# Attention rows of two steps turned together, and the first pair's second-layer weights asked for ahead of the half tile's

## The chip, the core and the metric

The kernel runs on one NeuronCore of a Trainium2 chip (trn2). The metric is the time of one execution in device microseconds. The core has five engines with queues of their own: PE (matrix products and transposes; PEld is its weight load), DVE (vector), ACT (scalar), POOL (gathers, scatters and some elementwise work) and SP (which here only asks for transfers). They meet through semaphores. All data are float32 but for some routing tables.

## The reference, cut to what matters

Lightning attention over 4 sequences of 768 tokens and 8 heads of 64, followed by a mixture of 8 experts with one expert per token. The router has a "locality gate": where it is at least one half, a token takes over the expert of the token before it.

```python
# attention, by blocks, with a decaying state per head
intra = einsum(einsum(qb, kb) * Dmask, vb)
inter = einsum(qb * lam_pow, kv_state)
out[sl] = intra + inter
kv_state = lam_block * kv_state + einsum(kb * rev_pow, vb)
# experts: x is the attention's output, 3072 rows of 512
e = argmax(logits) if s == 0 or local_gate < 0.5 else prev_e
h = maximum(x[b, s] @ w1[e], 0)        # 512 -> 1024
out[b, s] = softmax(logits)[e] * (h @ w2[e])   # 1024 -> 512
```

## The kernel before, in words

**Attention stage.** The work is cut into 24 steps of 128 tokens; step s belongs to sequence s % 4. The loop over s (lines 802 to 842) writes out by hand the order on PE, DVE, SP and POOL; ACT's order follows the program. A step does on PE, in this order: `scores(s + 1)` (products of keys and queries into ps0 and ps1; in a "wide" form, lines 196 to 201, with 8 products for the steps in WIDE, or in a "narrow" form, lines 202 to 209, with 16 smaller ones that leave out part of what the causal mask zeroes); `from_state(s)` (line 235, into po0 and po1; ACT then scales the state kv, line 239); `mix(s)` (line 248, also into po; ACT copies po to xc, line 251); `update(s)` (line 262, into pk0; DVE adds it to kv, line 265); and `rows_of(s - 1)` (line 272), which turns the 128 x 512 block of xc by four PE transposes into pk1, lets ACT copy that to a buffer xn (line 277) and asks for its writing to x_dram (line 281; the request is made by ACT, for the last three rows by SP). xc holds four steps, one for each sequence. DVE multiplies each step's scores by the mask (line 212, tile sm).

Between these stand pieces of routing. In every fourth step (s % 4 == 0) `gates` multiplies the last four blocks of xc with the router's weights into the PSUM tile pl, which ACT copies (line 289); in the step after it `logits` turns these (line 294) in pl. The PSUM tile pr serves the routing's own small products (`along_sequences`, `experts_of`, `ranks`, `by_slots`), each in a step named in the table `extras`. In the last step, `first_turned` (line 712) turns the first gathered tile through pr, and DVE copies it (line 713) for the first expert products.

**Expert stage.** First five tiles of 128 rows go one by one: `hidden` (line 731) and `output` (line 737). Then tiles of one expert are taken in pairs by a scheme of seven products per layer (a Strassen-like one): `product_1` (line 957) for the first layer, `product_2` (line 962) for the second, with sums of weights on DVE: `sums_1` of w1 and `sums_2` of w2 (lines 935 to 938). Within a pair DVE's sums_2 stand ahead of the sums of partial results (lines 1003 and 1004), and `product_1(c, ...)` after these writes the tile c that line 1004 reads. Half tiles (experts' rests of up to 64 rows) are woven into the pairs by "hooks": their first layer is line 1096, their second line 1118.

**Weights.** Each expert has 2 MB for either layer. Three buffers of either kind exist: w1t[0..2] and w2t[0..2]. The first pair uses number 1 (`w_of(0)`), the half tiles number 2, the second pair number 0. `weights_of(g, i, layers)` (line 682) loads tile g's expert into buffer i; the request is made by SP, in the order written: for a buffer still in use SP stands still until it is free, and with it all that comes after it on SP. w2t[1] is in use until `output(1, 1)` of tile 3 is through. w1t[2] is borrowed for routing values that `by_slots(1)` reads. The second pair's weights are asked for in hook 1 of the first pair (line 1205), the third pair's and the other half tiles' in later hooks.

Of the kernel before, what the change touches and what calls it, by code (L numbers as in the profile page):

```python
# [8 lines left out]
F32 = mybir.dt.float32  # L9
# [14 lines left out]
P = 128  # L24
B, H, S, DH = 4, 8, 768, 64
A = H // 2
DM = H * DH
# [11 lines left out]
PARTS = [(0, 8), (8, NA), (NA, NT)]  # L39
LOADS = 6  # L40
QUARTERS = [16, 17, 18, 19]
WIDE = [3, 4, 5, 6]
WARM = 10
KA = -(-(NA * P - E * (P - 1)) // P)

# [8 lines left out]
G2 = G1 + E  # L54
# [10 lines left out]
def kernel(  # L65
# [26 lines left out]
    def w1_src(e):  # L92
        return w1[bass.ds(e, 1)].rearrange("o (t p) f -> p (o t) f", p=P)
# [13 lines left out]
    pg = ctx.enter_context(tc.tile_pool(name="pg", bufs=1, space=PSUM))  # L107
# [78 lines left out]
    def scores(s):  # L186
# [8 lines left out]

        if s in WIDE:
            for a in range(A):
                for u in range(2):
                    rows = slice(DH * u, DH * u + DH)
                    nc.tensor.matmul(ps[u][:, a], lhsT=kt[rows, a], rhs=qt[rows, a],  # L200
                                     start=True, stop=True, skip_group_check=True)
        for a in range(A if s not in WIDE else 0):
            for j in range(2):
# [49 lines left out]
    def update(s):  # L253
        b, c = ORDER[s]
        x = inp.pop(s)
        if c + 1 < NC:
            kv, vn = kvs[b], x[:, 2].rearrange("p (a u d) -> p a u d", u=2, d=DH)
            kd = kds.pop(s).rearrange("p (a u d) -> p a u d", u=2, d=DH)
            pk = pg.tile([P, A, P], F32, name="pk0")[:, :, :DH]
            for a in range(A):  # L260
                for u in range(2):
                    nc.tensor.matmul(pk[DH * u:DH * u + DH, a], lhsT=kd[:, a, u], rhs=vn[:, a, u],  # L262
                                     start=True, stop=True, skip_group_check=True)
            if c:
                nc.vector.tensor_tensor(kv, pk, kv, ALU.add)
            else:
                nc.vector.tensor_copy(kv, pk)

    def rows_of(s):
        px = pg.tile([P, DM], F32, name="pk1")  # L270
        for a in range(A):
            nc.tensor.transpose(px[:, P * a:P * a + P], xc[:, a, ORDER[s][0]], ident)  # L272
        if s + 1 < NS:
            xn = att.tile([P, DM], F32, name="xn", bufs=4)
        else:
            xn = xlast
        nc.scalar.copy(xn, px)


        queue = nc.scalar if s + 3 < NS else nc.sync  # L280
        queue.dma_start(out=x_dram[P * s:P * s + P, :], in_=xn)
# [17 lines left out]
    pl = pg.tile([P, B * P], F32, name="pl")  # L299
    pr = pg.tile([P, DM], F32, name="pr")  # L300
# [381 lines left out]
    def weights_of(g, i, layers=(1, 2), cond=None, own=None):  # L682
        e = expert(g, own)
        if 1 in layers:
            nc.sync.dma_start(out=w1t[i], in_=w1_src(e), cond=cond, cond_hint=None if cond is None else True)
        if 2 in layers:
            nc.sync.dma_start(out=w2t[i], in_=w2_src(e), cond=cond, cond_hint=None if cond is None else True)

    def w_of(p):
        return (p + 1) % 2  # L690
# [94 lines left out]
    with tc.manual_schedule(engines={PE, DVE, SP, POOL}):  # L785

        warm = pg.tile([P, A, P], F32, name="pk0")
        for _ in range(WARM):
            nc.tensor.matmul(warm[:, 0], lhsT=ident, rhs=ident, start=True, stop=True)
        masks_of_lam()  # L790
        nc.gpsimd.memset(wgt, 0.0)
        constants_1()

        for s in range(LOADS - 1):
            inp[s] = load.tile([P, 4, DM], F32, name="inp")
        for s, half in ((0, 0), (1, 0), (0, 1), (1, 1), *((s, half) for s in range(2, LOADS - 1) for half in range(2))):
            nc.sync.dma_start(out=inp[s][:, 2 * half:2 * half + 2], in_=qkv[s][:, 2 * half:2 * half + 2])
        for s in range(3):
            prepare(s)
        scores(0)  # L800
        nc.sync.dma_start(out=wgt[:, :, :E + 1], in_=wg)
        for s in range(NS):
            if s + LOADS - 1 < NS:
                loaded(s + LOADS - 1)
            if s + 3 < NS and s != 1:
                prepare(s + 3)
            if s in QUARTERS:
                j = QUARTERS.index(s)
                nc.sync.dma_start(out=w1t[0][:, j], in_=w1_src(0)[:, j])
            if s == NS - 4:  # L810
                nc.sync.dma_start(out=w2t[0], in_=w2_src(0))
                weights(0)
            if s == NS - 1:
                nc.sync.dma_start(out=w1t[1], in_=w1_src(1))
                nc.sync.dma_start(out=w2t[1], in_=w2_src(1))
            if s + 1 < NS and s not in (1, 2, 3, 4, 5):
                scores(s + 1)
            from_state(s)
            if s % B == 1 and s > B:
                logits(s // B - 1)  # L820
            if s == 5:
                scores(6)
            extra_work(s, 0)
            if s % B == 0 and s:
                gates(s // B - 1)
            mix(s)
            if s == 0:
                update(0)
                query_powers(0)
            if s in (1, 2, 3, 4):  # L830
                scores(s + 1)
            if s == 1:
                query_powers(1)
                prepare(4)
                rows_of(0)
            if s:
                update(s)
            if s + 1 == NS:
                first_turned()
            if s > 1:  # L840
                rows_of(s - 1)
            extra_work(s, 1)
        x_ctx.close()
        act = ctx.enter_context(tc.tile_pool(name="act", bufs=2))
        w1t.append(act.tile([P, DT, F], F32, name="w1_2", bufs=1))
        w2t.append(act.tile([P, FT, DM], F32, name="w2_2", bufs=1))
        pools.append(act)

        pys.extend(pg.tile([P, DM], F32, name=f"pk{i}") for i in range(2))
        hq.update({(f, 1): act.tile([P, FT // 2, P], F32, name=f"h{f}1", bufs=1) for f in range(2)})  # L850
        xgh = act.tile([P, DM], F32, name="xgh", bufs=1)
        yt = act.tile([P, 2, DM], F32, name="y", bufs=1)
        xps = [act.tile([P, DT, P], F32, name=f"xp{i}", bufs=1) for i in range(3)]
        xs = act.tile([P, 3, DT // 2, P], F32, name="xs", bufs=1)
        s1 = act.tile([P, 3, DT // 2, F // 2], F32, name="s1", bufs=1)
        yl = s1[:, 0]
        s2 = act.tile([P, 3, FT // 2, DM // 2], F32, name="s2", bufs=1)
        hs = act.tile([P, 4, FT // 2, P], F32, name="hsum", bufs=1)
        part = act.tile([P, 3, FT // 2, P], F32, name="part", bufs=1)
        rest = act.tile([P, DM // 2], F32, name="rest", bufs=1)  # L860

        def finished(g):
            output(g % 2, g % 2)
            written(g, g % 2)

        def hiddens(g):
            hidden(g % 2, g % 2, 0)
            hidden(g % 2, g % 2, 1)


        xqs.extend((xlast, rt.tile([P, DM], F32, name="lg")))
        ahead(2, 0)
        xq = hq[1, 0].rearrange("p f i -> p (f i)")
        flipped(xq, xgt[1])
        ahead(3, 1)
        moved(xtt[1], xq, (0, 1))
        hidden(0, 0, 0)
        rows_of(NS - 1)
        weights(1)
        gates(NC - 1)  # L880
        moved(xtt[1], xq, (2, 3))
        hidden(0, 0, 1)
        by_slots(0, (2, 3, 4))
        logits(NC - 1)
        fresh_experts(2)
        flipped(xqs[1], xgt[0])
        ahead(4, 0)
        moved(xtt[0], xqs[1])
        finished(0)
        weights(2)  # L890
        along_sequences(2)
        flipped(xqs[0], xgt[1])
        hiddens(1)
        moved(xtt[1], xqs[0])
        experts_of(2)
        chances(2)
        flipped(xqs[1], xgt[0])
        finished(1)
        weights(3)
        ranks(2)  # L900
        masks(2)
        other_tiles()
        tokens_to_other_tiles()
        hiddens(2)
        moved(xtt[0], xqs[1])
        output(0, 0)
        weights(4)
        brought(1, (0, 1, 2, 3, 4))
        written(2, 0)
        hiddens(3)  # L910
        weights_of(KA, w_of(0), (1,))
        output(1, 1, range(FT // 2))
        by_slots(1, (0, 1, 2, 3, 4))
        weights_of(G2, 2)
        output(1, 1, range(FT // 2, FT))
        written(3, 1)

# [262 lines left out]
    with tc.manual_schedule(engines={PE, DVE, SP, ACTE}):  # L1180
        more, fulls, halves = (number(k, n) for k, n in enumerate((PMAX - PMIN + 1, E + 1, FIRST_SMALL + 1)))
        weights_of(KA, w_of(0), (2,))
        both_halves()
        pair_ahead(0)
        rows_out(1)
# [147 lines left out]
```

## Time and profile before

| what | value |
|---|---|
| median of 3 runs | 453.33 us (451.4 to 454.59) |
| the profiled execution's own time | 451.95 us |
| its span, first to last instruction | 450.1 us |
| granted TensorE clock | 0.994 |
| PE busy | 431.8 us (96%) |
| DVE, ACT, POOL busy | 62%, 45%, 24% |
| bytes moved | 124.85 MB, mean 277 GB/s |
| attention stage | up to about 102 us |
| five single tiles | about 103 to 178 us |
| pairs with half tiles | from about 178 us |

A line of the timeline gives start and length in microseconds, engine, source line, operation, what is written and read, a count, and in square brackets how long the engine stood idle before it and whom it waited for. "issue" is idle time in which the profile shows nothing waited for. In a line of PE, the start is exact and the end is modelled, so the pace is read from start to start. A line of the waits gives the sum, the number of times and the longest. Rows of busy tenths cut the span into 40 slices of 11.25 us.

### The profile page before, as it was taken

Reading aid. Unit: us, or ns where it says so; the run is one execution under the profiler, and the core shown is the slowest. Engines: PE = TensorE matmul, PEld = TensorE weight load, DVE = VectorE, ACT = ScalarE, POOL = GpSimd, SP = SyncE. Lnnn points to the kernel's source line nnn. Section 1 sums busy time; section 2 is a strip of 40 time slices with the busy share of each in tenths; the row PEclk is TensorE's granted clock in tenths of the full one; section 3 lists DMA queues with packets and bytes.
Section 4 is the critical chain, followed back from the end, with each engine's and each line's share of the span. In section 5 each row is a group of like instructions: output and inputs, shape, how many; then the busy total and the mean of one; then the engine's idle time right before and its main releaser. Section 6 shows DMA issues by size and latency. Waiting matters only on the chain.

```text
span 450.1 us, 10497 instructions
## 1 busy us (share of the span) xinstructions
PE 431.8 (96%) x4186; PEld 358.5 (80%) x4186; DVE 278.9 (62%) x562; ACT 201.7 (45%) x594; POOL 109.3 (24%) x120
## 2 busy tenths in 40 slices
PE   6999998899999999799999999999999999999993
PEld 5877786778667776788685999677799999898982
DVE  5547776871429949576463796100487888878661
ACT  2356665547454104543524448441445455556110
POOL 4476565231100041203220400110102011020101
PEclk9999999999999999999999999999999999999997
DMA  8999999979899899999994499997163838380101
GB/s 269 409 420 411 327 305 317 360 260 367 310 375 353 287 400 379 358 387 399 388 345 176 145 404 375 352 348 286 43 211 93 309 103 284 147 280 6 52 3 51
DMA packets 42575, 124.85 MB, mean 277 GB/s; under 512 B 3148, under 2 KB 3148, under 8 KB 40592
## 3 DMA queue, kind: packets, MB, share of 16 engines
q1 hardware_dynamic: 34976, 104.62, 63.4%
q0 software_dynamic: 4368, 13.90, 9.0%
q10 hardware_dynamic: 3168, 5.51, 3.2%
q8 instruction: 37, 0.61, 0.5%
q14 instruction: 26, 0.21, 0.1%
HBM read 124.02 MB, written 12.91 MB: 304 GB/s over the span
## 4 chain that ended last, share of the span: by engine, by line
PE 77%; DMA 12%; issue 6%; DVE 4%; POOLq 0%; POOL 0%
PE ps L731 11%; PE pk L962 11%; PE pk L737 11%; PE ps L957 10%; DMA out_dram<-y,sidxp 6%; PE po L248 5%; DMA w<-in_w_dram 5%; PE po L957 5%; PE pl L962 4%; PE ps L208 3%; PE pk L272 3%; PE pk L262 2%; PE po L235 2%; PE pr L1118 2%; PE pr L1096 2%
## 5 line engine op out<-in xcount | busy, mean ns | idle before, releaser
L731 PEld LDWEIGHTS ps<-xt,w 128*128 128x128 f32 x512 | 58.2, 192 | 3.0 <-issue 2.3
L731 PE MATMUL ps<-xt,w 128*128 128x128 f32 x512 | 59.1, 276 | 0.3 <-DVE xt L713 0.3
L737 PE MATMUL pk<-w,h 128*128 128x512 f32 x128 | 56.5, 593 | 0.0
L737 PEld LDWEIGHTS pk<-w,h 128*128 128x128 f32 x128 | 23.6, 190 | 26.3 <-issue 25.6
L703 POOL DMA_INDIRECT xg<-x_dram,gidx x25 | 25.8, 1032 | 59.2 <-DVE lg L717 27.7
L746 POOL DMA_INDIRECT out_dram<-y,sidx x14 | 14.0, 1001 | 105.8 <-DVE y L763 46.5
L212 DVE TENSOR_TENSOR sm<-ps,mask 128x512 f32<-128x512 f32 x46 | 29.7, 685 | 15.1 <-PE ps L208 7.6
L724 ACT COPY xp<-xlast 32x128 f32<-32x128 f32 x128 | 37.8, 295 | 1.7
L733 ACT ACTIVATE h<-ps 128x512 f32<-128x512 f32 x16 | 9.6, 597 | 57.6 <-PE ps L731 57.6
L724 ACT COPY xp<-lg 32x128 f32<-32x128 f32 x112 | 33.0, 295 | 2.6
L763 DVE TENSOR_SCALAR y<-pk,gate 128x512 f32<-128x512 f32 x8 | 5.9, 743 | 42.1 <-PE pk L737 30.4
L957 PEld LDWEIGHTS ps<-xp,w 128*128 128x128 f32 x256 | 30.5, 192 | 1.7 <-issue 1.3
L177 POOL TENSOR_TENSOR qd<-inp,lamq 128x512 f32<-128x512 f32 x20 | 25.6, 1278 | 24.9 <-PE po L235 11.4
L957 PE MATMUL ps<-xp,w 128*128 128x128 f32 x256 | 31.3, 275 | 0.0
L957 PE MATMUL ps<-xs,s 128*128 128x128 f32 x256 | 31.2, 275 | 0.0
L962 PE MATMUL pk<-w,h 128*128 128x256 f32 x128 | 30.5, 381 | 0.0
L962 PE MATMUL pk<-s,hsum 128*128 128x256 f32 x128 | 30.3, 380 | 0.0
L248 PE MATMUL po<-sm,inp 128*64 128x128 f32 x384 | 27.7, 280 | 2.5 <-DVE sm L212 1.6
L957 PEld LDWEIGHTS ps<-xs,s 128*128 128x128 f32 x256 | 29.9, 192 | 0.0
L248 PEld LDWEIGHTS po<-sm,inp 128*64 128x64 f32 x384 | 20.9, 136 | 9.5 <-issue 6.6
L962 PEld LDWEIGHTS pk<-s,hsum 128*128 128x128 f32 x128 | 23.9, 190 | 3.3 <-DVE s L1045 0.2
L962 PEld LDWEIGHTS pk<-w,h 128*128 128x128 f32 x128 | 23.5, 190 | 3.4 <-issue 0.6
(280 smaller groups left out, 792.0 us busy)
## 6 DMA issues: line engine op xcount, KB each, us to landing
w<-in_w_dram SPq DMA_DIRECT2D x43, 2048.0 KB, 11.4
inp<-in_qkv_dram SPq DMA_DIRECT2D x15, 1024.0 KB, 8.0
x_dram<-xn ACTq DMA_DIRECT2D x21, 256.0 KB, 7.2
inp<-in_qkv_dram SPq DMA_DIRECT2D x10, 512.0 KB, 7.7
inp<-in_qkv_dram SPq DMA_DIRECT2D x4, 768.0 KB, 6.3
w<-in_w_dram SPq DMA_DIRECT2D x4, 512.0 KB, 9.8
x_dram<-xn SPq DMA_DIRECT2D x2, 256.0 KB, 8.1
xg<-x_dram,gidx POOLq DMA_INDIRECT x25, 6.8
```

Of the source, the lines that this page charges most:

```text
L177: nc.gpsimd.tensor_tensor(qd, x[:, 0].rearrange("p (a i) -> p a i", i=P), lamq, ALU.mult)
L208: nc.tensor.matmul(ps[u][half, a, first:], lhsT=kt[rows, a, half], rhs=qt[rows, a, first:], start=True, stop=True, skip_group_check=True)
L212: nc.vector.tensor_tensor(sm[:, u], ps[u], mask[:, u], ALU.mult)
L248: nc.tensor.matmul(head(a, u), lhsT=vn[:, a, u], rhs=sm[:, u, a], start=(not c and a < 2), stop=True, skip_group_check=True)
L272: nc.tensor.transpose(px[:, P * a:P * a + P], xc[:, a, ORDER[s][0]], ident)
L703: nc.gpsimd.indirect_dma_start(out=xg, out_offset=None, in_=x_dram[:n, :], in_offset=bass.IndirectOffsetOnAxis(ap=gidx[i][:, j:j + 1], axi ...
L724: copy(xt[QP * j:QP * j + QP, :, QP * k:QP * k + QP], blocks[QP * k:QP * k + QP, :, j])
L731: nc.tensor.matmul(ph[:, j], lhsT=w1t[w][:, d, P * f:P * f + P], rhs=xtt[i][:, d], start=(d == 0), stop=(d == DT - 1))
L737: nc.tensor.matmul(pys[i], lhsT=hq[f // 4, i][:, f % 4], rhs=w2t[w][:, f], start=(f == 0), stop=(f == FT - 1))
L746: apart(nc.gpsimd.indirect_dma_start(out=out, out_offset=bass.IndirectOffsetOnAxis(ap=sidx[i][:, j:j + 1], axis=0), in_=y, in_offset=None, ...
L957: nc.tensor.matmul(to[:, m], lhsT=a[:, k, P * m:P * m + P], rhs=b[:, k], start=(new and not m and not k), stop=(k == 1), skip_group_check= ...
L962: nc.tensor.matmul(to, lhsT=a[:, f], rhs=b[:, f], start=(new and not f), stop=(f == FT // 2 - 1), skip_group_check=True)
```

## The change

Three edits. (1) `rows_of` is no longer called in every step from 2 on for the step before it; from step 3 on, every odd step calls it twice, for the two steps before it. The second call turns through pl (where s % 4 is 3) or pr (where s % 4 is 1) in place of pk1. In step 23 both calls stand ahead of `first_turned`, where the one call stood behind it. (2) Step 6 leaves WIDE, so its scores are taken in the narrow form. (3) The loads of the first half tile's weights (both layers, `weights_of(G2, 2)`) move behind the load of the first pair's second layer in SP's order.

```diff
-WIDE = [3, 4, 5, 6]
+WIDE = [3, 4, 5]
...
-    def rows_of(s):
-        px = pg.tile([P, DM], F32, name="pk1")
+    def rows_of(s, px=None):
+        if px is None:
+            px = pg.tile([P, DM], F32, name="pk1")
...
             if s:
                 update(s)
+            if s > 1 and s % 2:
+                rows_of(s - 2)
+                rows_of(s - 1, pl if s % B == 3 else pr)
             if s + 1 == NS:
                 first_turned()
-            if s > 1:
-                rows_of(s - 1)
             extra_work(s, 1)
...
         by_slots(1, (0, 1, 2, 3, 4))
-        weights_of(G2, 2)
         output(1, 1, range(FT // 2, FT))
         written(3, 1)
...
         weights_of(KA, w_of(0), (2,))
+        weights_of(G2, 2)
         both_halves()
```

## The prediction

> **What bounds the kernel now.** I read the page's rows of busy tenths first, then the list of waits, then the timeline around the largest wait of TensorE, then TensorE's timeline in the attention stage.
>
> ```profile
> PE   6999998899999999799999999999999999999993
> DMA  8999999979899899999994499997163838380101
> ```
>
> Each digit is 11.25 us. PE stands at 9 nearly everywhere, so what the end costs is PE's own work plus its few pauses. DMA is full up to slice 27 (about 300 us), so a transfer's place in the queue matters up to there. The list of waits shows which pauses of PE have a cause outside PE:
>
> ```profile
> PE po L957 <- DVE part L1004: 2.9, 1, 2.9
> ...
> DVE s L937 <- DMA w<-in_w_dram: 3.0, 1, 3.0
> ```
>
> There is one such pause of weight, and one wait of DVE for weights of the same size. The timeline of PE, then of DVE, shows that they are one event:
>
> ```profile
> 185.65 1.95 PE L957 MATMUL ps<-xp,w 128*128 128x128 f32 x16
> 190.54 2.05 PE L957 MATMUL po<-xs,w 128*128 128x128 f32 x16 [2.95 <-DVE part L1004]
> ```
>
> ```profile
> 186.09 1.22 DVE L937 TENSOR_TENSOR s<-w 128x1024 f32<-128x1024 f32 x1 [2.97 <-DMA w<-in_w_dram]
> 187.35 1.23 DVE L937 TENSOR_TENSOR w<-w 128x1024 f32<-128x1024 f32 x1
> 188.49 0.70 DVE L717 STREAM_TRANSPOSE lg<-xg 128x512 f32<-128x512 f32 x1
> ...
> 189.81 0.69 DVE L1004 TENSOR_TENSOR part<-part,po 128x512 f32<-128x512 f32 x1
> ```
>
> The first pair's sums of its second-layer weights (L937) stand on DVE ahead of L1003 and L1004; PE's next product overwrites what L1004 reads. The weights land at 186.09, because they are asked for last. The chain of waits gives the moment of asking and the wait; SP's timeline gives what went ahead:
>
> ```profile
> 164.55 21.52 DMA w<-in_w_dram
> ```
>
> ```profile
> 161.18 0.37 SPq L685 DMA_DIRECT2D w<-in_w_dram  x1
> 161.77 0.49 SPq L687 DMA_DIRECT2D w<-in_w_dram  x1
> ```
>
> These two are the half tile's 4 MB. The pair's 2 MB are asked for at 164.55, when PE has read the old ones, and land 21.5 us later.
>
> **Part 1, the order of the loads.** Afterwards SP holds at the pair's request until 164.55 and the half tile's two follow it. Ahead of the pair's is then only the request of 155.65. Counting the window's rates (207, 365, 438, 406, 356, 406 GB/s from 157 us, less 0.26 MB of rows written) its 2.1 MB are in at about 163. The same latency as for that one (about 1.9 us from request to flow, 155.65 to 157.5) makes the pair's flow from 166.4. At 0.4 MB per us and with two gathers beside it, it lands at about 173; DVE wants it at 183.1. The wait is gone by 10 us.
>
> DVE's row then runs 183.12 + 1.26 + 1.14 + 0.63 (the starts 186.09, 187.35, 188.49, 189.12) = 186.15; L1003 (0.69 to the next start) and L1004 (0.69) end at 187.53. PE is through at 185.65 + 1.95 = 187.60. **Gain 2.95 us**, whole, since no other PE pause lies up to 441 us.
>
> What is late next? The half tile's first product is at 198.21, its second at 203.94. From 166.4 the three loads with some 1.3 MB of gathers and rows are 7.6 MB, in by about 187. That is late by one microsecond against 186.07, but before, DMA ran dry at 184 to 187 (172, 291, 291 GB/s, some 1.1 us), which the longer queue fills. So the next loads land as before, while PE asks 2.95 us sooner. The tightest is the second half tile's first layer: before it is used at 215.21 (L1096), after at 212.26. From 166.4 to it lie seven loads (14.7 MB) and about 2.1 MB of gathers and rows, 16.8 MB. The 5 us windows from 165 to 210 average 382 GB/s: it lands at 210.4, 1.9 us in time. **Against this speaks** the Trainium skill, page "DMA: Bandwidth & Descriptors", section "Specifications", which gives about 358 GB/s as the HBM limit of one core: 16.8 MB would take 46.9 us, land at 213.3, and PE would wait 1.0 us of the 2.95. The windows here hold 340 to 411 GB/s and single microseconds over 420, so I take the measured rate: 0 lost, 1.0 as the far end.
>
> **Part 2, step 6's scores.** In the wide form they take 1.09 us of PE (chain: 27.94 to 29.04), in the narrow form 0.81 (31.11). The place is on PE's own path: **gain 0.28**. What it feeds, sm(6), is used only a step later.
>
> **Part 3, rows in pairs.** Eleven even steps (2 to 22) lose a group of four transposes, eleven odd ones (3 to 23) get a second one. PE's timeline:
>
> ```profile
> 32.31 1.09 PE L248 MATMUL po<-sm,inp 128*64 128x128 f32 x16
> 33.23 0.64 PE L262 MATMUL pk<-inp,kd 128*64 128x64 f32 x16
> 33.80 0.66 PE L272 MATMUL pk<-ident,xc 128*128 128x128 f32 x4
> 34.38 0.90 PE L208 MATMUL ps<-inp 64*64 64x128 f32 x32
> ```
>
> ```profile
> 101.36 0.66 PE L712 MATMUL pr<-ident,xg 128*128 128x128 f32 x4
> 101.85 0.60 PE L272 MATMUL pk<-ident,xc 128*128 128x128 f32 x4
> 102.79 3.84 PE L731 MATMUL ps<-xt,w 128*128 128x128 f32 x32 [0.34 <-DVE xt L713]
> ```
>
> Start to start a group costs 0.58; entering it from the 128*64 shape costs 0.11 more (L248 to L272 at 95.24 to 96.27 is 1.03, L248 to L262 is 0.92). Without it the change straight to 64*64 remains: 0.16 (11.43 to 12.51 is 1.08 against 0.92). An even step saves 0.58 + 0.11 - 0.16 = 0.53. A second group right behind one of the same shape costs 4 x 0.109 = 0.44 (101.36 to 101.85 is 0.49, of which 0.05 belongs to the first spacing). Net 0.09 a pair, **1.0 us** for eleven. The Trainium skill, page "TensorEngine Tiling (Array Packing)", section "Key Properties", says that a change of tiling mode drains TensorE; by it one drain goes per pair, and at the full 0.17 that PEld idles at such a change it would be 1.9. I keep the starts, and 1.9 as the upper end.
>
> What this calls forth:
> - Step 23: first_turned now stands last, so nothing covers DVE's L713. Before, L712 to L731 took 1.43 with a group of 0.44 in it: **-0.44**.
> - Step 22: DVE runs without rest from 89.67; sm(23) ends at 99.83, PE would want it at 100.33 - 0.53 + 0.44 - 0.53 = 99.71 and gets it near 99.95: **-0.25**.
> - ACT: a copy and its DMA request hold it 0.59 and 0.33 us, and the request waits for the copy:
>
> ```profile
> 31.15 0.59 ACT L277 COPY xn<-pk 128x512 f32<-128x512 f32 x1 [0.61 <-PE pk L272]
> 31.76 0.33 ACTq L281 DMA_DIRECT2D x_dram<-xn  x1
> ```
>
> From the first transpose at 0, copy 1 runs 0.70 to 1.29, its request to 1.64, copy 2 from 1.74 to 2.33, its request to 2.68; the kv scalings (1.06) and xc copies (0.65) of the next step end at 4.46. PE wants po for from_state at 1.02 + 0.72 + 0.55 + 0.92 + 0.57 + 0.16 + 0.72 = 4.65: just in time. But gates (steps 4, 8) and along_sequences (10, 14) want pl or pr at 2.29 and get it near 2.43: 4 x 0.14, **-0.5**. The rows' later writes cost nothing: the gathers at 91.6 read rows of steps 0 to 11 alone, the next to read all rows start at 162. On SP the write of row 21 moves behind the loads of w1t[1] and w2t[1] (100.85, 101.82), which so start sooner.
>
> Sum of part 3: 1.0 - 0.44 - 0.25 - 0.5 = **-0.2** (ends -1.5 and +1.6).
>
> **The sum.** 2.95 + 0.28 - 0.2 = 3.0 us. Against the profiled execution's 451.95 us: 448.9. The median is 453.33, 1.38 longer. PE's pauses in that profile that hang on memory traffic are this wait (2.95) and pauses for "issue" in attention (1.41, 1.24, 0.49, 0.40, 0.25: 3.8 in all). If the extra time of the other runs is spread over them alike, 2.95 of 6.75 of it, 0.6 us, goes with the wait: 453.33 - 3.0 - 0.6 = **449.7 us**, 0.8% less.
>
> **Rivals.**
> - *Larger (0.24)*: the wait for w2 is longer in the runs than in the profile, or fewer of the issue pauses remain. For it: the runs spread over 3.2 us, and the wait hangs on a full DMA. If all of the 1.38 is the wait, and part 3 gives its switch savings without ACT's waits, 453.33 - 4.3 - 0.28 - 0.5 = 448.2.
> - *Handed on (0.14)*: the wait moves to the second half tile's weights or the second pair's. For it: DMA is full to 240 us and the slack was 1.9. Against: the dry spell at 184 to 187 shows room. Half the gain goes: 451.3.
> - *Nothing from part 1 (within the last)*: only if the pair's load still landed after 183.1, 10 us later than worked out.
> - *Slower (0.08)*: ACT, with two copies and two requests in a row, delivers po late in every even step. It is 0.1 us from doing so. A lateness of 0.3 us in each of eleven steps cancels the gain; 0.7 us makes it 453.33 - 3.0 + 7.7 = 458.0.
>
> **How the numbers follow.** Likeliest, as summed, 0.54, with 448.5 to 451.0 as its own range. The range 447.2 to 452.2 adds the larger gain and the handed-on wait and leaves out most of the slower case. A change of 1% is about what a measurement of this kernel can tell from none; the line is at 448.8. Under it are the larger case (0.24) and a quarter of the likeliest (0.14): 0.38. Above 457.9 lies 0.06 of the slower case. The rest is 0.56.
>
> **What would show it.** Right: no wait of DVE L937 for DMA near 183 and PE's L957 without a pause there; the transposes at L272 in groups of eight, each pair of steps about 0.1 us shorter; L200 with 48 matmuls in place of 64; first hidden (L731) at nearly the old time, 102 to 103. Wrong: a new wait of PE's L1096 or L1118 for w near 195 to 220, waits of L235 for ACT's xc copies, or of L286 and L411 for xn over 0.3 us; the issue pauses gone or doubled would make the sum wrong without touching its steps.

## The result, and the profile after

| kernel | median | runs | ratio to before, 95% interval |
|---|---|---|---|
| before | 453.04 us (448.88 to 457.67) | 20 | |
| after | 452.35 us (450.43 to 455.44) | 20 | 1.0011 [0.9988, 1.0034] |

The change made no difference that can be measured. The ratio is taken over the fast executions alone, so it need not be the ratio of the two medians. The forecast was 449.7 us; 452.35 lies just above its range, 447.2 to 452.2. The profiled execution took 452.56 us (span 450.8, clock 0.996), that of before 451.95.

PE's row of busy tenths differs from that of before in the attention stage and at the pair:

```profile
PE   8998889898999999999999999999999999999993
```

In the fourth to tenth slice (34 to 113 us) PE now has five eights where before had two; the seventeenth (180 to 191 us), a 7 before, is a 9. So time was won at the pair and lost in attention. First the place where it was won, on DVE and then on PE:

```profile
186.50 0.17 DVE L1206 COPY owner<-owner 1x38 int32<-1x38 int32 x1
186.59 1.21 DVE L938 TENSOR_TENSOR s<-w 128x1024 f32<-128x1024 f32 x1
...
190.29 0.69 DVE L1005 TENSOR_TENSOR part<-part,po 128x512 f32<-128x512 f32 x1
```

```profile
189.20 1.95 PE L958 MATMUL ps<-xp,w 128*128 128x128 f32 x16
191.03 2.05 PE L958 MATMUL po<-xs,w 128*128 128x128 f32 x16
```

L938 (L937 before) starts straight behind the operation ahead of it, where it had stood 2.97 us for w; the second group of L958 shown here starts 1.83 us after the first, where it had been 4.89 us. SP's timeline shows the new order: the pair's second layer (L688) at 168.10, then the half tile's two loads.

```profile
168.10 0.37 SPq L688 DMA_DIRECT2D w<-in_w_dram  x1
169.04 0.37 SPq L686 DMA_DIRECT2D w<-in_w_dram  x1
169.62 1.64 SPq L688 DMA_DIRECT2D w<-in_w_dram  x1
```

From the first `hidden` product (L731 before, L732 after) to that second group it is 190.54 - 102.79 = 87.75 us before and 191.03 - 106.35 = 84.68 after: 3.07 less, where 2.95 was summed. But the first `hidden` product came at 106.35, 3.56 us late, though attention's first `mix` had begun 0.97 earlier (8.53 against 9.50). The attention stage grew from 93.29 to 97.82 us, by 4.5. PE's waits in that stage (sum, times, longest) name what it stood for:

```profile
PE pk L262 <- issue: 1.5, 1, 1.5
PE po L235 <- issue: 1.4, 1, 1.4
PE po L248 <- issue: 1.4, 2, 1.2
PE ps L208 <- issue: 1.4, 2, 1.2
PE po L235 <- ACT xc L251: 1.3, 2, 1.1
PE pk L262 <- DVE kv L265: 0.9, 1, 0.9
PE ps L732 <- DVE xt L714: 0.9, 1, 0.9
```

Two kinds of loss: pauses for "issue", 5.7 us in all where before had 3.8, and three waits for ACT and DVE, 3.1 us, of which before had only the last, at 0.34. (A listed pause is about 0.3 us shorter than the gap from one product's start to the next, since the ends are modelled.)

### The profile page after: what moved, and what is told of

The parts are those of the page before. It is cut to its first block, busy times and chain, and to the rows that moved or that the text cites. A ratio compares the mean times of both kernels' runs of the same rounds, so it can differ in the third digit from the quotient of the medians.

```text
span 450.8 us, 10530 instructions
## 1 busy us (share of the span) xinstructions
PE 431.9 (96%) x4202; PEld 359.5 (80%) x4202; DVE 278.6 (62%) x562; ACT 200.3 (44%) x594; POOL 109.2 (24%) x120
## 4 chain that ended last, share of the span: by engine, by line
PE 76%; DMA 12%; issue 6%; DVE 1%; SPq 1%; POOLq 0%; ACTq 0%; ACT 0%; POOL 0%; DVEq 0%
PE ps L732 13%; PE pk L738 12%; PE ps L958 12%; PE pk L963 11%; DMA out_dram<-y,sidxp 6%; PE po L958 5%; PE pl L963 4%; PE po L248 4%; DMA w<-in_w_dram 4%; PE ps L208 3%; DMA inp<-in_qkv_dram 2%; PE pr L1119 2%; PE pr L1097 2%; PE pk L262 2%; PE po L235 2%
## 5 line engine op out<-in xcount | busy, mean ns | idle before, releaser
L732 PEld LDWEIGHTS ps<-xt,w 128*128 128x128 f32 x512 | 58.2, 192 | 3.5 <-issue 2.3
L732 PE MATMUL ps<-xt,w 128*128 128x128 f32 x512 | 59.1, 276 | 0.9 <-DVE xt L714 0.9
L958 PEld LDWEIGHTS ps<-xp,w 128*128 128x128 f32 x256 | 30.4, 192 | 1.9 <-issue 1.7
L958 PE MATMUL ps<-xp,w 128*128 128x128 f32 x256 | 31.4, 276 | 0.0
L958 PE MATMUL ps<-xs,s 128*128 128x128 f32 x256 | 31.2, 275 | 0.0
L958 PEld LDWEIGHTS ps<-xs,s 128*128 128x128 f32 x256 | 29.9, 192 | 0.0
L248 PE MATMUL po<-sm,inp 128*64 128x128 f32 x384 | 27.7, 280 | 1.7 <-issue 1.4
L248 PEld LDWEIGHTS po<-sm,inp 128*64 128x64 f32 x384 | 21.1, 136 | 9.2 <-issue 7.5
```

The source lines that it names most:

```text
L248: nc.tensor.matmul(head(a, u), lhsT=vn[:, a, u], rhs=sm[:, u, a], start=(not c and a < 2), stop=True, skip_group_check=True)
L732: nc.tensor.matmul(ph[:, j], lhsT=w1t[w][:, d, P * f:P * f + P], rhs=xtt[i][:, d], start=(d == 0), stop=(d == DT - 1))
L958: nc.tensor.matmul(to[:, m], lhsT=a[:, k, P * m:P * m + P], rhs=b[:, k], start=(new and not m and not k), stop=(k == 1), skip_group_check= ...
```

## The experiments

Theory A, from these lines: the loads' order is worth what was forecast, and the rows in pairs lose it in attention by the three waits. Rival B: the loads' order is worth less in the run of executions than in one profile. Rival C: the narrow form of step 6, or the mere number of PE instructions, lengthens the issue pauses. In the table, "all" is the three edits together. Ratios are to before, run beside each kernel.

| kernel | what it holds | median | ratio, 95% interval | issue pauses in attention, profiled |
|---|---|---|---|---|
| e1_loads_only | loads | 447.86 | 0.9921 [0.9895, 0.9948] | 3.1 us |
| g1_loads_only_again | loads | 447.50 | 0.9900 [0.9874, 0.9925] | 2.7 |
| e3_narrow_only | narrow | 453.02 | 1.0012 [0.9987, 1.0036] | 6.0 |
| e4_loads_narrow | loads, narrow | 450.25 | 0.9960 [0.9937, 0.9984] | 3.4 |
| g2_loads_narrow_again | loads, narrow | 449.71 | 0.9946 [0.9926, 0.9967] | 5.1 |
| e2_pairs_only | pairs | 455.44 | 1.0087 [1.0054, 1.0121] | 3.5 |
| h1_loads_pairs_wide | loads, pairs | 450.99 | 0.9964 [0.9946, 0.9983] | 4.6 |
| g3_loads_pairs_to_17 | loads, pairs up to step 17 | 448.84 | 0.9928 [0.9903, 0.9953] | 3.8 |
| e5_pairs_to_17 | all, pairs up to step 17 | 451.03 | 0.9969 [0.9946, 0.9992] | not read |
| e6_requests_sp | all, late requests on SP | 451.71 | 0.9978 [0.9954, 1.0001] | 5.1 |
| e7_turned_first | all, first_turned first | 451.81 | 0.9978 [0.9956, 1.0001] | 5.1 |
| g4_pairs_mended | all, both mendings | 451.92 | 1.0003 [0.9980, 1.0026] | 6.2 |
| e8_qd4 | all, four buffers qd | 452.79 | 1.0009 [0.9985, 1.0034] | 5.4 |
| h2_loads_narrow_5 | loads, step 5 narrow | 449.09 | 0.9930 [0.9908, 0.9953] | 4.7 |
| h3_loads_wide_7_for_6 | loads, 6 narrow, 7 wide | 447.81 | 0.9909 [0.9878, 0.9940] | 1.1 |
| h4_loads_wide_to_7 | loads, 3 to 7 wide | 449.75 | 0.9937 [0.9914, 0.9961] | not read |

The profiled executions of e5 and h4 each hold a stretch of 6.8 us at half of TensorE's clock in attention (their mean granted clock is 0.988 and 0.987, the others' 0.994 and more), so no times are read from them. That of e1 holds 3.4 us at half clock, from 1.6 us behind its longest issue pause (1.63 us) on: there the products of L248 start 0.20 us apart in place of 0.10. Each entry of the last column is one execution's, and the same kernel on another chip gave 3.4 and 5.1 us (e4 and g2), so it is a weak witness by itself.

### Each part alone

e1 moves the one line of the loads, e2 makes the edits of `rows_of` and of its calls, e3 sets `WIDE = [3, 4, 5]`, and e4 is e1 and e3 together; each starts from the kernel before.

```diff
# e1 and e4
-        weights_of(G2, 2)
         output(1, 1, range(FT // 2, FT))
...
         weights_of(KA, w_of(0), (2,))
+        weights_of(G2, 2)
# e3 and e4
-WIDE = [3, 4, 5, 6]
+WIDE = [3, 4, 5]
# e2
-            if s > 1:
-                rows_of(s - 1)
+            if s > 1 and s % 2:
+                rows_of(s - 2)
+                rows_of(s - 1, pl if s % B == 3 else pr)
```

> The kernel before with the order of the loads alone changed. Theory A (paired rows lengthen the attention stage by what the loads win): attention ends near 102.8 us as before, no wait of DVE for w near 183, PE's pause of 2.95 us gone; about 2.9 us less than before, ratio 0.993 to 0.995. Theory B (the win of the loads is handed on to later waits in every run): the pause moves to L1096, L1118 or a later sum of weights, ratio 0.998 to 1.001.

> The kernel before with the rows in pairs alone. Theory A: 3 to 4 us more than before, ratio 1.006 to 1.009, the attention stage longer by as much, w2 still waited for. Theory C (PE's pauses for issue happen to be longer in the profiled execution; the pairs cost nothing by themselves): ratio 0.998 to 1.002.

> The kernel before with step 6's scores in the narrow form alone. Theory A: 0.3 us less, not to be told from none, ratio 0.998 to 1.001. Theory D (the 32 more instructions of the narrow form bring more pauses for issue): 1 to 3 us more, ratio 1.002 to 1.006.

> Both edits but not the pairs. Theory A: the fastest of these, 2.9 to 3.3 us less than before, ratio 0.992 to 0.995. Theory B or D: between 0.997 and 1.003.

The loads alone win 0.8% (453.0 x 0.0079 = 3.6 us); B falls. The pairs alone lose 0.9% (3.9 us). The narrow form alone can't be told from nothing, but on top of the loads it costs 0.9960 - 0.9921 = 0.4%, about 0.35% either way. What was handed on of the loads' gain is small: from the first `hidden` product to the last instruction it is 347.3 us before, and 344.4 to 344.6 in e1, in g1 (e1 on another chip) and in the kernel after. The waits of e1's PE after attention hold one line for weights, at the tightest place that the prediction named (L1096 there, L1095 in this kernel):

```profile
PE pr L1095 <- DMA w<-in_w_dram: 0.2, 1, 0.2
```

The waits of e2 carry the first pair of tiles' old wait and the three of the kernel after, so these three belong to the rows in pairs:

```profile
PE po L959 <- DVE part L1006: 3.0, 1, 3.0
PE po L235 <- ACT xc L251: 1.2, 2, 1.0
...
PE pk L262 <- DVE kv L265: 0.9, 1, 0.9
PE ps L732 <- DVE xt L714: 0.9, 1, 0.9
```

The old wait can cost more than its own length. In e2 TensorE's granted clock fell at its end, to a mean of 0.68 from 190 to 195 us (the last number but two in the second view), and the group of products that followed took 3.34 us from start to start; in the profile of before, without that fall, it took 1.89 (190.54 to 192.43):

```profile
192.10 3.50 PE L959 MATMUL po<-xs,w 128*128 128x128 f32 x16 [2.96 <-DVE part L1006]
195.44 1.95 PE L959 MATMUL ps<-xp,s 128*128 128x128 f32 x16
```

```profile
190.00:195.00 5.00, 2.90 (x13) 2.90 (x14) 4.37 (x6) 1.11 (x2) 1.01 (x1) 0.68 1.02 392
```

The granted clocks of all executions fit that: their mean is 0.992 to 0.993 in each set of the kernel before, 0.995 in e1 and 0.996 in g1. The difference, about 0.0035, times 450 us is about 1.5 us, an estimate of what the loads' order wins beyond the wait itself. No run took the wait away alone and left the clock, so this part is argued.

### Where the pairs lose: steps 18 to 23

ACT's timeline of the kernel after, in steps 21 and 22, and PE's wait that follows from it:

```profile
98.41 0.23 ACT L478 ACTIVATE kd<-kd 128x32 f32<-128x32 f32 x1 [3.01 <-DVE kd L477]
98.55 0.63 ACT L251 COPY xc<-po 128x256 f32<-128x256 f32 x2
99.06 0.60 ACT L278 COPY xn<-pk 128x512 f32<-128x512 f32 x1
99.54 0.61 ACT L278 COPY xn<-pr 128x512 f32<-128x512 f32 x1
99.69 1.92 ACTq L282 DMA_DIRECT2D x_dram<-xn  x2
101.66 0.65 ACT L251 COPY xc<-po 128x256 f32<-128x256 f32 x2 [1.51 <-PE po L248]
```

```profile
102.18 0.84 PE L235 MATMUL po<-qd,kv 64*64 64x128 f32 x16 [1.14 <-ACT xc L251]
```

ACT stood idle for 3 us ahead of the routing's L478 (before: 2.15), so the copy of step 21 and the two copies of the pair came to it at once. Its two requests (ACTq) lie from 99.69 to 101.61: the second, at 100.51, took 1.10 us, where each one in the kernel before took 0.33 to 0.35. The next step's copy to xc, which PE's L235 waits for, stood behind them.

The second wait is DVE's. The lines of the kernel after around step 18:

```profile
86.70 1.28 POOL L177 TENSOR_TENSOR qd<-inp,lamq 128x512 f32<-128x512 f32 x1 [1.48 <-issue]
86.73 1.26 DVE L509 TENSOR_SCALAR owner<-own 1x5 int32<-1x5 f32 x1
87.92 0.40 DVE L265 TENSOR_TENSOR kv<-pk,kv 128x256 f32<-128x256 f32 x1
...
88.47 0.69 PE L262 MATMUL pk<-inp,kd 128*64 128x64 f32 x16 [0.94 <-DVE kv L265]
```

An operation on five elements took 1.26 us, and ended with a POOL product that had begun 0.03 us before it. (The Trainium skill, page "SBUF — State Buffer", section "SBUF: two separate sides", describes a port pair that POOL and some DVE operations hold in turn for a whole instruction; this case agrees with it.) In the kernel before the same operation (L508 there) took 0.16, and POOL's product came 2 us later:

```profile
84.24 0.16 DVE L508 TENSOR_SCALAR owner<-own 1x5 int32<-1x5 f32 x1
86.36 1.28 POOL L177 TENSOR_TENSOR qd<-inp,lamq 128x512 f32<-128x512 f32 x1 [3.64 <-PE po L235]
```

Five kernels take these causes away: the late pairs; the last requests on ACT; first_turned behind the transposes; POOL's product at that moment; and the second and third together (g4).

```diff
# e5: the kernel after, single rows from step 18 on
-            if s > 1 and s % 2:
+            if 1 < s < 18 and s % 2:
...
+            if s > 17:
+                rows_of(s - 1)
# e6 and g4
-        queue = nc.scalar if s + 3 < NS else nc.sync
+        queue = nc.scalar if s + 7 < NS else nc.sync
# e7 and g4: first_turned ahead of the pair
+            if s + 1 == NS:
+                first_turned()
             if s > 1 and s % 2:
# e8
-            qd = qds[s] = att.tile([P, A, P], F32, name="qd", bufs=3)
+            qd = qds[s] = att.tile([P, A, P], F32, name="qd", bufs=4)
```

> The changed kernel with pairs only up to step 17, single rows from 18 on as before. Theory E (what the pairs cost is three waits of the last steps: PE's L262 for DVE's kv in step 19, L235 for ACT's xc in steps 21 and 22, L732 for first_turned last in step 23): these waits go, the early pairs win 0.1 us each, about 3 us less than the changed kernel and the level of the loads with the narrow form, ratio 0.992 to 0.996 to the kernel before. Theory G (each pair costs, wherever it stands): two thirds of the loss stay, 0.999.

> The changed kernel with the requests for writing rows 17 to 20 made by SP in place of ACT. If ACT's second request, which lasts 1.1 us in step 21 where one lasts 0.33, is what makes xc late, L235's wait of 1.1 us in step 23 goes and nothing comes in its place: about 1.1 us less than the changed kernel, ratio 0.997 to 0.999. If the two copies in a row are enough to make xc late: half of the wait stays. SP could hold up the quarter loads while it waits for a copy; then w1t[0] would be late at L732.

> The changed kernel with first_turned ahead of the two rows in step 23. L732's wait for DVE's L714 goes from 0.85 us to none, since eight transposes (0.88) lie under it: 0.85 us less than the changed kernel, ratio 0.998 to 1.000 to the kernel before. If this place is of no account, 1.001.

> The changed kernel with four buffers for qd in place of three, so that POOL's product of step 22 can start sooner than at from_state. If DVE's 5-element L509 lasts 1.26 us because POOL's product runs in the same time, L509 is back at 0.16 us, the kv sum in time and L262's wait of 0.94 us gone: 0.9 us less than the changed kernel, ratio 0.998 to 1.000. If L509 is slow for another reason it stays at 1.26.

> The changed kernel with both mends of the last steps: first_turned ahead of the rows of step 23, and the requests for rows 17 to 20 by SP. If their two effects add, 1.5 to 2.5 us under the changed kernel, 0.995 to 0.998, with L262's wait for kv in step 19 as the only one of the three that stays.

Without the late pairs the ratio goes from 1.0011 to 0.9969: 0.42% back, with an interval of about 0.3% on the difference. In e6 ACT has no request between its copies, and PE's wait falls from 1.14 to 0.40:

```profile
98.83 0.59 ACT L278 COPY xn<-pr 128x512 f32<-128x512 f32 x1
100.93 0.65 ACT L251 COPY xc<-po 128x256 f32<-128x256 f32 x2 [1.50 <-PE po L248]
```

In e7 the two groups of transposes cover DVE's copy, and L732 starts without a wait. e8 moves POOL's product to 84.70 and 88.65, and the small operation is short again, as it is in g4, where POOL's product began 0.4 us behind it:

```profile
87.49 0.16 DVE L509 TENSOR_SCALAR owner<-own 1x5 int32<-1x5 f32 x1
```

So each cause is shown at its place. The times say less. e6 and e7 are each 0.33% under the kernel after, about as much as the interval of that difference; g4, with both, can't be told from it; and e8's time is unchanged: its profile has two waits that the kernel after did not have (L412 for ACT, 0.7; L620 for DVE's L610, 0.4). The wait in e7 for ACT also fell, to 0.34, with no edit for it: of its two requests there the second took 0.33 us, not 1.10. Why g4 didn't add the two gains stays open; its issue pauses were the longest of these, 6.2 us.

### The parts again, and the early pairs

g1 and g2 are e1 and e4 on another chip; g3 is e1 with pairs of rows in steps 3 to 17 only.

```diff
# g3: e1 with
+            if 1 < s < 18 and s % 2:
+                rows_of(s - 2)
+                rows_of(s - 1, pl if s % B == 3 else pr)
...
-            if s > 1:
+            if s > 17:
                 rows_of(s - 1)
```

> The order of the loads alone, once more, beside the three below on one chip. Theory A: 0.992 to 0.995 as before, the fastest or level with the loads and early pairs.

> Loads and narrow form, once more, to tell whether the narrow form costs. Theory H (its 32 more instructions cost some 1 to 2 us by PE's pauses for issue, since 0.9921 and 0.9960 stood against each other): 0.003 to 0.004 above the loads alone. Theory A (it wins 0.28 us): level with them within 0.002.

> Loads, and pairs up to step 17 only, step 6 wide. If the early pairs win 0.09 us each as forecast, 0.7 us under the loads alone, ratio 0.991 to 0.993; if they are worth nothing, level; if they cost by themselves, 0.995 or more.

The loads are confirmed (0.9900), and so is the cost of the narrow form: 0.9946 - 0.9900 = 0.46%, about 0.33% either way. The eight early pairs stand at 0.9928, 0.2% above the mean of e1 and g1 (0.9910), within the interval of that difference (about 0.3%). Their switches do save time, counted from the starts in the trace of the kernel after: an even step goes from `update` to `scores` in 0.56 us, where it took 0.56 + 0.59 with the transposes between, and an odd step's eight transposes take 1.02 where four took 0.59. That is 0.59 - 0.43 = 0.16 a pair. But the first pair (rows of steps 1 and 2) loses. From the scores in step 2 (L200) to the gates of step 4 it is 21.37 - 14.93 = 6.44 us in g1 and 22.62 - 15.54 = 7.08 in g3:

```profile
14.93 1.16 PE L200 MATMUL ps<-inp 64*128 64x128 f32 x16
21.37 1.06 PE L286 MATMUL pl<-xc,wgt 128*32 128x512 f32 x8
```

```profile
15.54 1.16 PE L200 MATMUL ps<-inp 64*128 64x128 f32 x16
17.52 0.40 PE L248 MATMUL po<-sm,inp 128*64 128x128 f32 x2 [0.21 <-issue]
22.62 1.07 PE L287 MATMUL pl<-xc,wgt 128*32 128x512 f32 x8
```

In step 2 the transposes had stood between the scores of step 3 and its mix, and so had covered DVE's mask products for that mix; without them PE pauses at L248. And the gates, which want pl, come 0.80 us after L235 in place of 0.60. So the eight pairs save 7 x 0.16 - 0.64, about 0.5 us (0.1%), which g3's time can't show; its issue pauses were 3.8 us in the profile, those of e1 and g1 2.9 on average.

### Is it the narrow form or the number of instructions?

PE's issue pauses in g1 and in g2, as its waits list them:

```profile
PE po L248 <- issue: 1.7, 2, 1.1
PE pk L262 <- issue: 1.1, 2, 0.7
```

```profile
PE pr L411 <- issue: 1.6, 1, 1.6
PE pk L262 <- issue: 1.3, 1, 1.3
PE po L235 <- issue: 1.0, 1, 1.0
PE po L248 <- issue: 0.9, 2, 0.5
PE ps L208 <- issue: 0.3, 1, 0.3
```

They are longer with the narrow form, and stand at other lines. I counted PE's products in the trace, where each product of the program stands as two, from the program's start up to each such pause. (A gap is from one product's start to the next, about 0.05 to 0.1 us where nothing is waited for.)

| kernel | products in all | products ahead of the gap (gap in us) |
|---|---|---|
| before | 4186 | 597 (0.47), 849 (0.68), 1352 (1.68), 1604 (1.48), 1731 (0.76) |
| g1 | 4186 | 597 (0.95), 849 (1.39), 1478 (0.56), 1731 (0.80) |
| g2 | 4202 | 598 (0.66), 723 (0.58), 849 (1.77), 1227 (1.54), 1479 (0.80), 1731 (1.26) |
| after | 4202 | 597 (1.69), 974 (1.44), 1100 (1.70), 1352 (0.46), 1478 (1.46) |
| h1 | 4186 | 597 (1.49), 723 (0.85), 974 (0.56), 1100 (1.41), 1478 (1.39) |

In every build they lie on one grid with a step of 126 products: 597, 723, 849, 975, 1101, 1227, 1353, 1479, 1605, 1731 and so on, give or take one. (Only pauses of under 0.3 us stand elsewhere, as the one at product 232 in g3, shown above.) So the pauses belong to places in PE's instruction stream, not to the work done there. The profile's table of DMA queues lists a queue of kind "instruction":

```profile
q8 instruction: 37, 0.61, 0.5%
```

37 packets of 16,384 bytes; the 4202 products are 33 steps of 126. The Trainium skill, page "Runtime: NRT & Kernel Launch", section "Instruction fetch mechanics", says that each engine's instructions are refilled in blocks of 16 KiB, 256 instructions, while it works on the block before, and that crossing into a new block is mostly hidden. 126 products with 126 weight loads are 252 instructions, which leaves four for whatever else PE's queue holds: the step and the packets agree with the page, "mostly hidden" does not, with four to six gaps of over 0.4 us in each of these builds at the eleven crossings from product 597 to 1857.

The trace also has each packet's time. One packet of that queue belongs to each crossing, and every pause ends a set time behind it. In the kernel after:

| products ahead | packet on q8, us | next product starts | packet's end to that product | gap |
|---|---|---|---|---|
| 597 | 34.52 to 35.59 | 37.10 | 1.51 | 1.69 |
| 723 | 39.80 to 40.89 | 42.87 | 1.99 | 0.05 |
| 974 | 52.91 to 53.86 | 55.32 | 1.46 | 1.44 |
| 1100 | 59.33 to 60.20 | 61.78 | 1.58 | 1.70 |
| 1352 | 70.88 to 71.82 | 73.28 | 1.47 | 0.46 |
| 1478 | 78.22 to 79.16 | 80.55 | 1.39 | 1.46 |

The third row in the views (the packet is the only one of its queue from 52.91 to 53.86):

```profile
q8 instruction: 1, 0.02, 6.2%
```

```profile
55.32 0.79 PE L208 MATMUL ps<-inp 64*64 64x128 f32 x27 [1.17 <-issue]
```

In the five builds of the table above, all 25 pauses end 1.23 to 1.58 us behind their packet's end, and at none of the 55 crossings does PE go on sooner than 1.17 us behind it. So the pauses are PE waiting for its next block of instructions. What differs is when the packet starts: 2.9 to 5.0 us after the crossing before in front of a pause, 0.8 to 4.2 us elsewhere; the transfer itself takes 0.9 to 1.5 us. Then 16 products more in step 6 need not cost by themselves: they shift all later work against the grid. Four kernels test that.

```diff
# h1: the kernel after with
+WIDE = [3, 4, 5, 6]
# h2: e1 with
+WIDE = [3, 4, 6]
# h3: e1 with
+WIDE = [3, 4, 5, 7]
# h4: e1 with
+WIDE = [3, 4, 5, 6, 7]
```

> The changed kernel with step 6 in the wide form again: loads order and pairs without the narrow form. If the narrow form costs 0.4% by itself wherever it stands, this is 0.997 of before (1.001 less 0.004) and PE's pauses for issue in the attention stage sum to 3 to 4 us in place of 5.7. If the narrow form only changes how the pairs fall, or its cost was scatter, the ratio stays at 1.000 to 1.001.

> Loads order, and step 5 in place of step 6 in the narrow form. As many products as with step 6 narrow. If the cost hangs on the number of PE instructions (16 products and 16 weight loads more), the ratio is 0.995 as with step 6, and the issue pauses are as long. If it hangs on what step 6 feeds or stands beside, it is 0.990 to 0.991.

> Loads order, step 6 narrow and step 7 wide: as many PE instructions as before, moved by one step. If the cost hangs on the number of instructions, 0.990 to 0.991 as with the loads order alone, issue pauses 2.7 to 3.1 us. If it is step 6's narrow form in its place, 0.995.

> Loads order, steps 3 to 7 wide: 16 products and 16 weight loads fewer than before. If fewer instructions shorten the pauses further, 0.987 to 0.989; if only PE's products count, step 7 costs 0.28 us more and the ratio is 0.991 to 0.992; if the pauses jump with where instructions come to stand, either may come, with pauses that differ from both.

h3 keeps step 6 narrow, and 4186 products: 0.9909, the level of the loads alone (0.9910). Its waits show the shortest pauses of all, at two places of g1:

```profile
PE po L248 <- issue: 1.1, 2, 0.6
```

So the narrow form of step 6 costs nothing in itself that these runs can tell (about 0.35% either way). h2 has 4202 products with another step narrow: its pauses stand at the very products of g2 (723, 849, 1227, 1479, 1731). Its ratio, 0.9930, lies between the two levels and can't be told from either. h1 shows that the 16 products cost the changed kernel the same: 1.0011 - 0.9964 = 0.47%, about 0.3% either way. h4 warns against a simple rule: 16 products fewer than before are not faster still but 0.9937, where the products' own price gave 0.991 to 0.992; it can't be told from the loads alone. It is where the grid falls that seems to count, not how many instructions there are. Why the packet of some blocks starts 3 or 4 us later than that of others, the runs do not show; none changed the traffic beside them alone.

## Why the prediction was wrong

| part | forecast | measured |
|---|---|---|
| loads' order | -2.95 us (-3.55 with the other runs' spread) | -3.6 and -4.5 (e1, g1) |
| narrow form | -0.28 | +1.8, +2.1 and +2.1 (e4 over e1, g2 over g1, after over h1) |
| pairs | +0.2 | +2.4 (h1 over e1 and g1), +3.9 (e2) |

A gain of 0.9% and two losses of about 0.5% cancel. (That they add up to the measured +0.1% is no test: each is the step from one of these kernels to the next, from before over the loads and h1 to the kernel after.) The forecast went wrong at two steps: Part 2's "The place is on PE's own path: gain 0.28", and Part 3's sum of switch savings and waits.

- **Part 1 was right** in place, mechanism and size. The waits of L937 and L957 are gone. The executions beyond the profiled one win somewhat more; the forecast had put 0.6 us there, by a spread over PE's pauses, and the granted clocks suggest about 1.5. Handing on was 0 to 0.6 us in single profiles (L1095: 0.2 in e1, 0.6 in e4, nothing in the kernel after), less than the 1.0 that would follow from the HBM limit in the Trainium skill, page "DMA: Bandwidth & Descriptors", section "Specifications".
- **Part 2 failed in its scope.** Step 6 does save what was read from PE's starts: in the step that holds these scores it is 4.41 us from one `update` to the next in e1, and 4.14 in e4. But the step "The place is on PE's own path: gain 0.28" counts products' time alone. The same edit adds 16 products and 16 weight loads to PE's stream (x4186 to x4202), and the issue pauses go with the stream. I had listed these pauses (3.8 us) and used them only to spread the other runs' extra time. Its own sign of being wrong, "the issue pauses gone or doubled would make the sum wrong without touching its steps", names the place: they were not doubled, but 5.7 us. In the profiles they account for some 1.3 us of the 2 (2.9 us on average in e1 and g1, 4.2 in e4 and g2); a lower mean granted clock, by 0.0008 to 0.0015, would by estimate be another 0.4 to 0.7.
- **Part 3, the switch savings**, came out at the size forecast, by luck: ten pairs save 0.16 us each, where 0.09 was summed, and the first pair loses 0.64, which was not foreseen. That makes 1.0 us, the forecast's figure, of two errors. The direct change to the 64*64 shape, taken at 0.16, costs nothing (L262 to L208 takes 0.56, as long as L262 to L272 before).
- **Part 3, ACT, was mis-sized.** "Copy 1, its request, copy 2, its request" ending at 2.68 is not the order that ACT took: the second copy ran ahead of the first request, which by itself is sooner; but the second request took up to 1.10 us, not 0.33. "Just in time" for po was right after eight of the ten pairs that a `from_state` with such a wait follows; after the last two of them ACT had idled ahead of L478, and PE waited 0.18 and 1.14 us. The rival that ended slower named this mechanism, but in each step at 0.3 us or more. Of the 4 x 0.14 for gates and along_sequences only the gates of step 4 came later, by 0.20 us (part of the first pair's loss), and the 0.25 of step 22, for sm(23), did not show.
- **Part 3, step 23** was right: L732's wait went from 0.34 to 0.85, 0.51 more (forecast 0.44).
- **Part 3, not foreseen**: POOL's and DVE's collision at L509, 0.94 us. The three waits make 1.14 + 0.94 + 0.51 = 2.6 us, less 1.0 of savings 1.6, of the +2.4 measured. The rest is less than what h1's issue pauses are longer (1.7 us: 4.6 against 2.9 on average in e1 and g1). The two together are 3.3 us and lie within the interval of the 2.4, about 1.2 us either way, but rest on single profiles; how much of the loss is waits and how much pauses stays open.

The best version is the loads' order alone: 0.9921 and 0.9900 of before.

## What to carry to other kernels

An edit that is priced by its instructions' time has a second price where an engine is fed close to its limit: look for pauses that nothing explains, count the instructions up to them, and compare builds with the same count before you judge a form by half a per cent. Work that is gathered to save switches arrives on the next engines in bursts; price it where these engines are already late (here the last three of eleven pairs cost about 0.4%), not on average. The order in which one queue asks for transfers was the cheapest edit and the only one whose gain stayed, because the profile showed one wait with one cause.

## What the runs showed of the hardware

- PE's pauses for "issue" stand on a grid of 126 products with their weight loads, in every build; one of them was 1.6 us (g2, L411), and their sum ran from 1.1 to 6.2 us in builds that differ by 16 products and some order. In five builds each of the 25 pauses ended 1.23 to 1.58 us after a packet of 16,384 bytes on the instruction queue had ended.
- At the end of a wait of about 3 us (e2), and 1.6 us after an issue pause of 1.63 us (e1), TensorE's clock was granted at half for 3.4 us; after an issue pause of 1.70 us in e6, and the wait of 2.95 us in the profile of before, it was not.
- A DVE operation on five elements took 1.26 us in place of 0.16 while a POOL product ran, and ended with it.
- Of two requests of 256 KB in a row on ACT's queue, the second took 0.33 us in one build (e7, step 21) and 1.10 in another (the kernel after), where single ones in the kernel before took 0.33 to 0.35.
- Single executions of one kernel spread by about 1% either way (before: 448.88 to 457.67 us), so steps under half a per cent needed some twenty runs each, and several here are still not told apart.
